# Which queue loads the second sequence's first keys and queries, and which one issues the last store

## The chip, the cores and the metric

The kernel runs on one core of one Trainium2 chip. A core has five engines with an instruction queue each: PE (TensorE: matrix products, into PSUM), DVE (VectorE), ACT (ScalarE), POOL (GpSimd) and SP (SyncE, which here only issues DMAs). DMAs are issued from SP and from POOL; a DMA issued from POOL can round fp32 to bf16 on its way, one from SP copies bytes as they are. The metric is the device time of one execution in microseconds, the median of several runs.

## The reference

Attention that looks at the best six key chunks of each query, followed by a two-layer network with a squared ReLU. Shapes: 4 sequences, 8 heads, 768 positions, 64 wide; network 512 to 2048 to 512.

```python
def _attn_ref(q, k, v):
    k_chunks = k.reshape(B, H, nc, chunk, D)              # nc = 24 chunks of 32 keys
    k_min, k_max = np.min(k_chunks, axis=3), np.max(k_chunks, axis=3)
    ub = np.sum(np.maximum(q[..., None, :] * k_min[:, :, None],
                           q[..., None, :] * k_max[:, :, None]), axis=-1)
    ub = np.where(causal, ub, -1e9)
    top_chunks = np.argsort(ub, axis=-1)[..., -6:]
    scores = scale * np.matmul(q, k.transpose(0, 1, 3, 2))
    ...
    scores = np.where(chosen & causal_mask, scores, -1e9)
    attn = softmax(scores)
    return np.matmul(attn, v)

def _moe_ref(x, w_in, w_out):
    h = np.maximum(x @ w_in, 0.0)
    return h * h @ w_out
```

`_attn_ref` and `_moe_ref` are cut here to what matters.

## The kernel before

**How the work is cut.** Each sequence is cut into blocks of 128 positions. The first block of every sequence has at most four chunks of keys in sight, so that it needs no selection; `first_transposes` and `first_attention` do it for all eight heads of a sequence at once. These four first blocks, one of each sequence, then go through the network together: `up(f, 0, 256, f)` for sequences 0 and 1, `up(f, 256, 512, f)` for 2 and 3, each for the first four column groups of w_in, then the rest. The other five blocks go by pairs of heads (16 pairs, `stage_a` for transposes, bounds and the choice of chunks, `stage_b` for scores and values, and other forms for the last sequence), and each sequence's five blocks then go through the network (`ffn`).

**What sets the order.** `Plan` takes every piece of work as an operation with a due date, the engines that could do it with an assumed cost each (`plan.op({"ACT": 0.48}, due, ...)`), what it needs, and the buffers it uses. `Plan.order` runs through time in a small model of the engines and of the transfers: among the operations that could start first it takes the one with the earliest due date, notes engine and start, and in the end writes all of them out in order of start. So the assumed costs and the times at which engines are first free (`free`) decide which engine does what and in which order; on the chip each engine then works its own list off in that order, and waits where an input is late. Where the model expects PE to wait in the opening, it writes filler products on the tile `warm`. Due dates come from formulas and from a list `moves` of shifts, each for a range of operations by number, that stands in `P`.

**The loads.** `P["sp"]` names the loads issued from SP, `'K0 Q0 K1 Q1'`: first blocks of keys and queries of sequences 0 and 1. `load_by_sp` (L496) loads them in fp32 into the tile `raw` (L500) and rounds them with a copy by DVE or ACT (L503, shown by the profile at the helper's L370). All other loads are issued from POOL by `load`, which rounds on the way: `load_first` (L461) for first blocks, `load_pair` (L553, shown at L555) for one head's other blocks, `load_w_in` (L560) for weights. Their list is `P["loads"]`: capital letters are first blocks (K2: keys of sequence 2), `k0` is a pair's keys, two loads, `i0` a quarter of w_in. `P["order"]` permutes the single loads of this list; the order issued is Q3, K2, V1, K3, V0, Q2, i0, V2, V3, then single loads of pairs. POOL issues a load only if the load eight before it has landed.

**Before the first load.** POOL makes `ident` (the identity for transposes) and `ahead` (a causal mask) and may set columns of ones in `vn` (`ones`, L520). `made["rows", 0]` (ACT, L432) writes rows that index the key chunks; `made["rows", 1]` to `[..., 7]` are copies of these by whichever engine is free (`kq_rows`, L429: POOL at L437, DVE and ACT by the helper `copy`, L368 and L370). With `after=1` in `P`, the first load is made to need the first of these copies:

```python
    if P["after"]:
        plan.loads[0].needs.append(made["rows", P["after"]])
```

**The stores.** `down` (L1189) makes one block's output `py`, copies it to `ob` (L368 or L370), and stores it (L1213) from SP, or from POOL for sequences 1 and 2. The last block is cut into columns 0 to 384 and 384 to 512, so that the last store is short.

Of the kernel before, what the change touches and what calls it, by code (L numbers as in the profile page):

```python
# [13 lines left out]
ACT = mybir.ActivationFunctionType  # L14
# [67 lines left out]
class Plan:  # L82
# [12 lines left out]
    NEVER = 1e9  # L95

# [22 lines left out]
    def order(self):  # L119
        free = {e: 0.7 for e in ("PE", "ACT", "DVE", "POOL", "SP")}  # L120
# [10 lines left out]
        landed, done, loads = [], [], 0  # L131
        rows = 128
        dma = Transfers()
        while ready:
# [34 lines left out]
            if engine == "PE":  # L169
# [9 lines left out]
                rows = op.rows  # L179
            op.engine, op.start, op.end = engine, st, st + cost  # L180
# [37 lines left out]
def kernel(  # L218
# [32 lines left out]
             -1393.33, -782.42, -326.54], sp='K0 Q0 K1 Q1', rows=[-2963.23,  # L251
             -1559.78, 780.78, -565.55, 1811.92, 457.36, -1818.66, -283.78],
             after=1, up_due=-65.96, up_rate=8.56, half=4, due=[-23.17,
# [3 lines left out]
             sel=2, loads='Q3 K3 V0 V1 Q2 K2 i0 V2 k0 V3 q0 i1 k1 v2 q1 i2 '  # L257
             'v0 i3 k2 q2 o1 o0 v1 o2 k3 o3 v3 q3')
    P.update(moves=[(702, 770, 14.04), (644, 759, -9.08), (940, 964, 20.66), (410,
# [1053 lines left out]
```

## Time and profile before

| what | us |
|---|---|
| median of 3 runs | 261.64 (261.3 to 263.74) |
| the profiled execution | 262.89 |
| its span, first to last instruction | 261.2 |
| SP's loads of queries and keys into raw, issue to landing, median | 4.0 and 4.4 |
| POOL's loads of w_in in the first 25 us, issue to landing, median | 7.7 |
| POOL's loads of v in the first 25 us, issue to landing, median | 6.7 |

The profile is that of one execution. A busy PE isn't PE at its peak, since products are pipelined and their ends modelled. Times in the order of time count from the span's start. A line such as L370 is that of the helper that records the instruction, so groups are told apart by their tiles: `q<-raw` is the rounding of SP's queries, `q<-in_q_dram` a load of a first block from POOL, `qn<-in_q_dram` one of a pair. DMA instructions show the time in which they are issued, not that of the transfer. PEclk 1.00 is the full clock.

### The profile page before, as it was taken

The page shows a single profiled execution, that of the slowest core. Times are in us where ns is not written, and L with a number is a line of the kernel's source. Part 1 is how long each engine was busy: PE and PEld are TensorE (multiplying, and loading weights), DVE is VectorE, ACT ScalarE, POOL GpSimd, SP SyncE. Part 2 cuts the span into 40 slices and gives each one's busy share as a digit, 9 for nine tenths or more (in the row PEclk, how much of TensorE's full clock was granted, in tenths as well). Part 3 has the DMA queues.
Part 4 walks back from the last instruction along what each step waited for, and adds up shares of the span by engine and source line. Part 5 has one row for each costly group of instructions (what it writes and reads, how often), then busy time and mean ns, then how long its engine had stood idle before and what let it go on. Part 6 is the DMA issues. An engine that isn't in the chain of part 4 may idle for free.

```text
span 261.2 us, 6709 instructions
## 1 busy us (share of the span) xinstructions
PE 249.4 (95%) x2471; PEld 160.3 (61%) x2471; DVE 191.0 (73%) x692; ACT 188.6 (72%) x379; POOL 115.2 (44%) x194
## 2 busy tenths in 40 slices
PE   6878899999999999999999999999999999999995
PEld 2547456666688666565678655656766554865443
DVE  6548999899999999998799972568979840555000
ACT  8545799685899999999988766776985821677112
POOL 7969988779758578832332031150003401000000
PEclk9599999999999999999999999999999999999999
DMA  8999999999999999991451753964797025200122
GB/s 157 138 159 148 168 181 169 183 139 183 170 211 137 145 109 173 152 166 23 77 163 28 162 74 94 207 116 103 175 184 118 17 72 136 82 0 4 40 80 80
DMA packets 117281, 32.16 MB, mean 123 GB/s; under 512 B 99840, under 2 KB 114944, under 8 KB 117248
## 3 DMA queue, kind: packets, MB, share of 16 engines
q0 software_dynamic: 75888, 15.73, 73.4%
q1 hardware_dynamic: 41360, 16.00, 31.4%
q8 instruction: 19, 0.31, 0.5%
q14 instruction: 14, 0.11, 0.2%
HBM read 32.77 MB, written 6.55 MB: 151 GB/s over the span
## 4 chain that ended last, share of the span: by engine, by line
PE 70%; DVE 11%; ACT 9%; DMA 4%; POOL 3%; issue 2%; ACTq 0%; POOLq 0%
PE py L1199 28%; PE ph L1168 25%; PE ps L1008 7%; PE av L1020 4%; ACT e L1032 4%; DMA v<-in_v_dram 4%; ACT kqc L368 4%; PE ps L1065 2%; DVE kqc L370 2%; PE av L1098 2%; DVE h L1186 2%; DVE kr L845 1%; DVE m L816 1%; DVE ht L1177 1%; POOL k L462 1%
## 5 line engine op out<-in xcount | busy, mean ns | idle before, releaser
L1168 PE MATMUL ph<-xT,w_in_sb 128*128 128x256 bf16 (+2 forms) x592 | 95.7, 304 | 1.7 <-DVE ht L1177 0.7
L1199 PE MATMUL py<-w_out_sb,h 128*128 128x512 bf16 (+2 forms) x400 | 91.6, 370 | 0.0
L1168 PEld LDWEIGHTS <-w_in_sb 128*128 128x128 bf16 x592 | 55.3, 97 | 25.9 <-issue 2.5
L1032 ACT ACTIVATE e<-ps 128x512 bf16<-128x512 f32 x120 | 64.9, 608 | 7.9 <-PE ps L1008 5.0
L1175 ACT ACTIVATE ht<-ph 128x384 bf16<-128x384 f32 (+2 forms) x120 | 53.3, 451 | 18.7 <-PE ph L1168 14.0
L1199 PEld LDWEIGHTS <-h 128*128 128x128 bf16 x400 | 36.2, 97 | 33.6
L1186 DVE TENSOR_TENSOR h<-ht 128x256 bf16<-128x256 bf16 (+2 forms) x148 | 47.6, 332 | 10.6 <-ACT ht L1175 8.2
L988 POOL TENSOR_SCALAR_AFFINE_SELECT e<-e 128x128 bf16<-128x128 bf16 (+1 forms) x66 | 24.4, 377 | 43.8 <-ACT e L1032 42.8
L1008 PE MATMUL ps<-kqc 88*128 88x128 bf16 (+1 forms) x240 | 39.4, 272 | 0.7 <-ACT e L1032 0.6
L368 ACT COPY ob<-py 128x512 f32<-128x512 f32 (+2 forms) x24 | 13.8, 575 | 29.2 <-PE py L1199 29.2
L1008 PEld LDWEIGHTS <-kqc 88*128 88x128 bf16 x240 | 19.8, 97 | 11.3 <-issue 1.1
L1020 PEld LDWEIGHTS <-e 128*128 128x128 bf16 x480 | 21.6, 97 | 4.5 <-POOL e L988 0.5
L1103 ACT ACTIVATE e<-ps 128x512 bf16<-128x512 f32 x40 | 21.5, 605 | 1.9 <-PE ps L1065 1.8
L1177 DVE TENSOR_SCALAR ht<-ph 128x256 bf16<-128x256 f32 (+2 forms) x28 | 13.7, 492 | 11.7 <-PE ph L1168 11.5
L1020 PE MATMUL av<-vn,e 128*128 128x65 bf16 x360 | 21.7, 193 | 0.0
L1213 POOL DMA_DIRECT2D out_dram<-ob x10 | 5.5, 553 | 33.8 <-ACT ob L368 33.8
L1112 DVE TENSOR_TENSOR e<-e,mask 128x512 bf16<-128x512 bf16 x40 | 17.4, 457 | 3.2 <-ACT e L1103 2.2
L716 DVE TENSOR_TENSOR x<-av,rc 128x320 bf16<-128x320 f32 (+1 forms) x40 | 18.6, 472 | 0.5
L988 POOL TENSOR_SCALAR_AFFINE_SELECT mask<-mask 128x256 bf16<-128x256 bf16 x20 | 9.2, 496 | 20.9 <-DVE x L716 12.5
L845 DVE TENSOR_REDUCE kr<-kT 128x24 bf16<-128x768 bf16 x16 | 14.8, 953 | 0.9 <-PE kT L373 0.8
L368 ACT COPY kqc<-sT 24x384 bf16<-24x384 bf16 (+1 forms) x27 | 11.7, 434 | 4.3 <-PE sT L373 2.6
L714 DVE RECIPROCAL rc<-av 128x5 f32<-128x5 f32 (+1 forms) x40 | 7.3, 187 | 9.4 <-PE av L1020 5.3
(115 smaller groups left out, 323.9 us busy)
## 6 DMA issues: line engine op xcount, KB each, us to landing
mask<-seen SPq DMA_DIRECT2D x16, 336.0 KB, 7.8
out_dram<-ob SPq DMA_DIRECT2D x13, 256.0 KB, 2.6
out_dram<-ob POOLq DMA_DIRECT2D x10, 256.0 KB, 2.9
w_in_sb<-in_moe_w_in_dram POOLq DMA_DIRECT2D x4, 512.0 KB, 7.6
w_out_sb<-in_moe_w_out_dram POOLq DMA_DIRECT2D x4, 512.0 KB, 9.0
vn<-in_v_dram POOLq DMA_DIRECT2D x15, 128.0 KB, 5.8
nt<-in_q_dram POOLq DMA_DIRECT2D x10, 128.0 KB, 6.1
nt<-in_k_dram POOLq DMA_DIRECT2D x10, 128.0 KB, 5.8
```

The lines of the kernel that those rows point to most:

```text
L368: nc.scalar.copy(dst, src)
L716: return plan.op({"DVE": 0.06 + 0.00108 * D * n}, due, lambda _: nc.vector.tensor_mul(x(), av[:, :, 0:D], rc[:, 0:n].unsqueeze(2).to_broad ...
L845: nc.vector.tensor_reduce(kr[:, mm].rearrange("d (t c) -> d t c", c=128 // CH) if b >= BY_DMA else kr[:, mm], part(kT).rearrange("d t (c j ...
L988: nc.gpsimd.affine_select(out=e, in_=e, compare_op=ALU.is_ge, fill=0.0, base=0, channel_multiplier=-1, pattern=[[0, n], [1, 128]])
L1008: nc.tensor.matmul(ps[:, 128 * c:128 * (c + nt)], lhsT=kqs(slice(0, KC), s, hh)[:, 128 * j:128 * (j + 1)], rhs=qss(slice(0, KC), s, hh)[:, ...
L1020: nc.tensor.matmul(av[:, t - 1], lhsT=e[:, 128 * c:128 * (c + 1)], rhs=value_tile(b, h, j), start=(i == 0 and c == 0), stop=(i == len(BANK ...
L1032: nc.scalar.activation(e.tile, ps.tile, ACT.Exp, scale=scale), [sc], [ps, e])
L1103: done = plan.op({"ACT": 0.48}, due + 0.5, lambda _: nc.scalar.activation(e.tile, ps.tile, ACT.Exp, scale=scale), [sc], [ps, e])
L1168: nc.tensor.matmul(ph.tile, lhsT=w_in_sb[:, ki, 128 * f:128 * (f + 1)], rhs=xT[:, c0 // 128:c1 // 128, ki], start=(ki == 0), stop=(ki == N ...
L1175: nc.scalar.activation(ht.tile, ph.tile, ACT.Relu)
L1186: {"DVE": 0.067 + w / 1920}, at[0] + P["h2"], lambda _: nc.vector.tensor_mul(h2[f][:, c0:c1], ht.tile, ht.tile), [op], [ht, h2[f]])))
L1199: nc.tensor.matmul(py.tile, lhsT=h2[f][:, 128 * t:128 * (t + 1)], rhs=w_out_sb[:, f, c0:c1], start=(f == 0), stop=(f == NFI - 1))
```

## The change

Keys and queries of sequence 1's first block (`K1`, `Q1`) go from SP's list to the head of POOL's, which rounds them on the way; their two copies on DVE or ACT go. `after=0`: the first load no longer needs a copy of the index rows. The last store is issued from ACT, the engine that can make the copy before it. The planner's assumptions are others: engines are first free at 0.8 to 2.0 us and not all at 0.7, the first two loads cost 0.34 and 0.18 us more, `ident`, `ahead` and `ubmask` have other costs, `wait` is 0.00419 and not 0.00328. `moves` and `order` are other lists, so the order of work is another on all engines, in the whole run. The order of loads becomes K1, Q1, Q3, V0, V1, K3, Q2, i0, K2, V3, one load of k0, V2, then single loads of pairs.

```diff
+    SLOW = (0.34, 0.18)
...
-        free = {e: 0.7 for e in ("PE", "ACT", "DVE", "POOL", "SP")}
+        free = {"PE": 0.9, "ACT": 2.0, "DVE": 0.9, "POOL": 1.0, "SP": 0.8}
...
+            if op.load and loads < len(self.SLOW):
+                cost += self.SLOW[loads]
...
-             -1393.33, -782.42, -326.54], sp='K0 Q0 K1 Q1', rows=[-2963.23,
+             -1393.33, -782.42, -326.54], sp='K0 Q0', rows=[-2963.23,
...
-             after=1, up_due=-65.96, up_rate=8.56, half=4, due=[-23.17,
+             after=0, up_due=-65.96, up_rate=8.56, half=4, due=[-23.17,
...
-             sel=2, loads='Q3 K3 V0 V1 Q2 K2 i0 V2 k0 V3 q0 i1 k1 v2 q1 i2 '
+             sel=2, loads='K1 Q1 Q3 K3 V0 V1 Q2 K2 i0 V2 k0 V3 q0 i1 k1 v2 q1 i2 '
...
-    P.update(moves=[(702, 770, 14.04), (644, 759, -9.08), (940, 964, 20.66), (410,
+    P.update(moves=[(698, 766, 15.28), (638, 753, -8.79), (938, 962, 18.75), (677,
...
-             order=[0, 5, 3, 1, 2, 4, 6, 7, 10, 9, 19, 12, 11, 8, 13, 14, 15, 16,
+             order=[0, 1, 2, 4, 5, 3, 6, 8, 7, 12, 11, 9, 21, 14, 13,
...
-             wait=0.00328)
+             wait=0.00419)
...
-    made["ident"] = plan.op({"POOL": 0.75}, -997, lambda _: make_identity(nc, ident))
-    made["ahead"] = plan.op({"POOL": 0.55}, -994, make_ahead)
+    made["ident"] = plan.op({"POOL": 0.60}, -997, lambda _: make_identity(nc, ident))
+    made["ahead"] = plan.op({"POOL": 0.45}, -994, make_ahead)
...
-    made["ubmask"] = plan.op({"DVE": 0.8}, -997, make_ubmask)
+    made["ubmask"] = plan.op({"DVE": 1.27}, -997, make_ubmask)
...
-            plan.op({"POOL": 0.80} if by_pool else {"SP": 0.35}, at[0] + 1, lambda e: (
-                nc.gpsimd if e == "POOL" else nc.sync).dma_start(
+            by = {"POOL": 0.80} if by_pool else {"ACT": 0.10} if c0 else {"SP": 0.35}
+            plan.op(by, at[0] + 1, lambda e: {
+                "POOL": nc.gpsimd, "ACT": nc.scalar, "SP": nc.sync}[e].dma_start(
                     out[rows[t]:rows[t] + 128, c0:c1], ob.tile), [op], [ob],
                 packets=2 * w, turns=not by_pool, free=by_pool)
```

Between `moves=` and `order=` both lists run on for dozens of lines of shifts.

More of the change, by code (lines that the diff above doesn't have):

```diff
@@ L256 @@
              'q3 v2 v3 k3', shift={}, p0=-2735.84, wait=0.01, xt=(1, 2, 3),
-             sel=2, loads='Q3 K3 V0 V1 Q2 K2 i0 V2 k0 V3 q0 i1 k1 v2 q1 i2 '
+             sel=2, loads='K1 Q1 Q3 K3 V0 V1 Q2 K2 i0 V2 k0 V3 q0 i1 k1 v2 q1 i2 '
              'v0 i3 k2 q2 o1 o0 v1 o2 k3 o3 v3 q3')
-    P.update(moves=[(702, 770, 14.04), (644, 759, -9.08), (940, 964, 20.66), (410,
[69 rows of a table removed]
-             order=[0, 5, 3, 1, 2, 4, 6, 7, 10, 9, 19, 12, 11, 8, 13, 14, 15, 16,
[4 rows of a table removed]
-             wait=0.00328)
+    P.update(moves=[(698, 766, 15.28), (638, 753, -8.79), (938, 962, 18.75), (677,
[110 rows of a table added]
+             463, -2.42)], order=[0, 1, 2, 4, 5, 3, 6, 8, 7, 12, 11, 9, 21, 14, 13,
[5 rows of a table added]
+             wait=0.00419)
     nc.scalar.preload_act_table_set("natural_log_exp_and_others")
```

188 rows, old and new, of tables (order, sel) are left out of this document.

## The prediction

> **What bounds the kernel now.** I read the page first, then busy time by stage, PE's waits, and the order of time of the opening.
>
> ```profile
> PE 249.4 (95%) x2471; PEld 160.3 (61%) x2471; DVE 191.0 (73%) x692; ACT 188.6 (72%) x379; POOL 115.2 (44%) x194
> PE 70%; DVE 11%; ACT 9%; DMA 4%; POOL 3%; issue 2%; ACTq 0%; POOLq 0%
> ```
>
> The first line is busy time, the second the chain that ended last. PE is busy for 249.4 of 261.2 us and carries 70% of the chain. A part of the change that doesn't give PE its work earlier, or shorten what stands behind PE's last matmul, gives nothing. Where PE has room is seen by stage; the first number of a row after the comma is PE's busy time, then PEld, DVE, ACT, POOL; the granted clock, the DMA share and GB/s end it.
>
> ```profile
> 0.00:3.80 3.80, 2.67 (x7) 1.02 (x8) 2.47 (x19) 2.95 (x4) 2.26 (x11) 1.00 0.49 111
> 3.80:7.20 3.40, 1.60 (x12) 0.56 (x10) 2.56 (x6) 3.26 (x5) 3.34 (x6) 1.00 1.50 208
> 7.20:10.60 3.40, 2.90 (x30) 1.85 (x31) 1.56 (x4) 1.68 (x4) 3.40 (x5) 0.54 2.09 133
> 10.60:14.00 3.40, 3.40 (x36) 2.55 (x36) 2.41 (x9) 1.07 (x2) 3.40 (x5) 0.50 1.68 145
> 14.00:17.40 3.40, 2.74 (x34) 1.71 (x32) 1.62 (x5) 2.17 (x4) 2.53 (x3) 0.96 1.74 161
> 17.40:20.80 3.40, 1.91 (x22) 1.60 (x23) 0.83 (x4) 0.77 (x2) 1.38 (x2) 1.00 2.09 153
> 20.80:24.20 3.40, 3.05 (x47) 2.65 (x46) 3.12 (x12) 2.37 (x5) 3.40 (x5) 1.00 1.64 177
> 24.20:130.00 105.80, 103.10 (x1106) 67.82 (x1105) 100.06 (x357) 93.23 (x183) 75.47 (x120) 1.00 1.70 149
> 130.00:258.00 128.00, 127.98 (x1191) 80.53 (x1188) 76.38 (x282) 80.83 (x173) 20.03 (x43) 1.00 0.44 97
> 258.00:261.20 3.20, 0.06 (x2) 0.00 (x0) 0.00 (x0) 0.27 (x1) 0.00 (x0) 0.82 0.24 82
> ```
>
> Up to 24.2 us PE is idle for 24.2 - 18.27 = 5.9 us, and for 6.8 us it runs at half clock. From 24.2 to 130 it is idle for 105.80 - 103.10 = 2.70 us, with VectorE at 100.06 beside it. From 130 to 258 nothing is left, and the last 3.2 us are the last store. So there is an opening, a middle with 2.7 us to give, and a tail.
>
> ```profile
> PE T L373 <- DVE q L370: 2.0, 2, 1.2
> PE sT L373 <- DVE selb L875: 0.8, 1, 0.8
> ```
>
> Two of PE's waits (us in total, times, longest): the largest of the opening is for VectorE's rounding of queries that SP loaded, the other is the largest of the middle. The opening in order of time (start, length, what, and in brackets the idle time before) shows two more waits of PE, for Pool's loads:
>
> ```profile
> 2.91 0.90 SPq L500 DMA_DIRECT2D raw<-in_k_dram  x1
> 1.59 0.29 POOL L413 TENSOR_SCALAR_AFFINE_SELECT ahead<-ahead 128x128 bf16<-128x128 bf16 x1
> 1.83 0.45 POOL L523 MEMSET vn<- 128x40 bf16 x2
> 3.07 0.82 POOL L437 TENSOR_SCALAR_AFFINE_SELECT kqc<-kqc 24x768 bf16<-24x768 bf16 x1 [0.79 <-ACT kqc L432]
> 4.02 1.20 POOL L462 DMA_DIRECT2D q<-in_q_dram  x1
> 5.21 1.04 POOL L462 DMA_DIRECT2D k<-in_k_dram  x1
> 6.25 0.88 POOL L462 DMA_DIRECT2D v<-in_v_dram  x1
> 9.71 0.80 POOL L562 DMA_DIRECT2D w_in_sb<-in_moe_w_in_dram  x1
> 6.56 0.82 DVE L370 CAST q<-raw 128x512 bf16<-128x512 f32 x1 [0.78 <-DMA raw<-in_q_dram]
> 7.72 0.53 DVE L370 CAST k<-raw 128x512 bf16<-128x512 f32 x1 [0.34 <-DMA raw<-in_k_dram]
> 8.85 0.61 PE L685 MATMUL ps<-t,t 64*128 64x128 bf16 x8
> 16.17 0.83 PE L641 MATMUL ph<-warm 128*128 128x256 bf16 x6
> 17.49 1.05 PE L1168 MATMUL ph<-xT,w_in_sb 128*128 128x256 bf16 x8 [0.49 <-DMA w_in_sb<-in_moe_w_in_dram]
> 19.94 0.40 PE L692 MATMUL av<-v,e 128*128 128x65 bf16 x8 [1.41 <-DMA v<-in_v_dram]
> ```
>
> Pool waits 0.79 us for ScalarE's first index rows, copies a set of them (0.82 us), and only then issues loads, one behind the other, from 4.02 us. The first weights are its seventh load; PE takes them at 17.49 us, with 0.83 us of filler on warm and 0.49 us of idleness before.
>
> **The change part by part.**
>
> Pool's first load, not held back: Pool ends ahead at 1.59 + 0.29 = 1.88 us, so the first load can start at 1.9 us, 2.1 us earlier. The index rows and the memsets that it did before (0.82 and 0.45) go to ScalarE or VectorE, or between the loads, where each delays every later load by its length.
>
> Two loads moved from SP to Pool: SP issues two of its four, Pool two more, ahead of all others. The first two loads cost 1.20 and 1.04 us whichever they are, later ones 0.88. The weights are then the eighth: 1.9 + 1.20 + 1.04 + 5 x 0.88 = 8.5 us instead of 9.71: 1.2 us earlier, or 0.4 if the copy of rows (0.82) stands between. Behind this the transfers must keep up:
>
> ```profile
> q1 hardware_dynamic: 1738, 0.44, 132.9%
> q0 software_dynamic: 2373, 0.30, 234.9%
> raw<-in_q_dram SPq DMA_DIRECT2D x2, 256.0 KB, 4.0
> q<-in_q_dram POOLq DMA_DIRECT2D x2, 128.0 KB, 4.3
> k<-in_k_dram POOLq DMA_DIRECT2D x2, 128.0 KB, 4.5
> ```
>
> The first two rows are packets in 4 to 6 us (SP's queue alone) and in 9 to 11 us (Pool's alone): 869 a microsecond against 1187. Two tensors of some 1024 packets take 2.36 us there and 1.73 here: 0.6 us less. The lead that weights and later loads get lies between 0.6 (transfers) and 1.2 us (issues); I take 0.9, their middle, as the two limits alternate.
>
> The Trainium skill speaks against this part: its page "DMA: Bandwidth & Descriptors", section "Issuing engine by pattern", gives simple loads to Sync as the generally faster issuer, and its section "Issuing engines are not separate DMA queues" says that another issuer saves only issue time, because all run on the same 16 engines. By that rule the sum would lose the 0.6 and, where Pool's issues aren't what limits, the lead. The trace agrees in the time to landing (4.0 against 4.3 us) and not in packets per microsecond, where SP's hold 253 bytes each (0.44 MB by 1738) and Pool's 126.
>
> VectorE's two casts go, 0.82 + 0.53 = 1.35 us. The second sequence's queries are ready at 7.38 and its keys at 8.25 us now; by Pool they are issued at 1.9 and 3.1 us and land, at 4.3 to 4.5 us each, at about 6.3 and 7.5 us. That moves the second sequence's transposes, and the scores of 8.85 us that stand behind them in PE's order, up by some 0.8 us. It is worth nothing by itself: the cover is the wait for weights at 17.49, over 8 us later. If that cover were gone it would be worth the 0.8.
>
> The new order of loads is read from the two lists; these rows price what it moves:
>
> ```profile
> 15.84 0.40 PE L685 MATMUL ps<-t,t 64*128 64x128 bf16 x8
> 8.96 0.42 DVE L370 COPY t<-T 128x512 bf16<-128x512 bf16 x1 [0.71 <-PE T L373]
> 16.27 1.09 ACT L701 ACTIVATE e<-ps 128x512 bf16<-128x512 f32 x2 [1.15 <-PE ps L685]
> 21.05 0.53 PE L692 MATMUL av<-v,e 128*128 128x65 bf16 x8
> 22.48 0.44 PE L373 MATMUL qT<-ident,qn 128*128 128x128 bf16 x5
> ```
>
> In the new order the third sequence's keys go from second place to behind the first weights, and its values behind those and a load of the pairs. Keys need more steps than values before an output: transposes, copy, scores, exponentials, some 2.35 us by 0.44, 0.42, 0.40 and 1.09 us. At the place where values land now (PE's wait ends at 19.94), less 0.9, they land at 19.0 and reach their values product at about 21.4, against 21.05 for the last of these products now (an estimate from these rows). So the second half of the first up-projection gains nothing, while the pairs, which keep their distance from the start of the stream, gain the 0.9; with them starts the first chain of bounds and selection, which ends in PE's 0.8 us wait for selb.
>
> Opening: -0.9, from -1.2 to +0.5 where the keys come late.
>
> The middle: due dates and costs of the planner are replaced, so the order of work on all engines changes, which no row shows. Below lies at most the 2.70 us of idleness; above, an order that fits badly can lose as much. Of the rows, the 0.8 us wait for selb is nearest to this change, since its chain starts with the loads: I take half of it, -0.4.
>
> The last store on ScalarE:
>
> ```profile
> 258.14 0.27 ACT L368 COPY ob<-py 128x128 f32<-128x128 f32 x1 [0.41 <-PE py L1199]
> 258.43 0.33 SPq L1213 DMA_DIRECT2D out_dram<-ob  x1
> ```
>
> ScalarE's copy ends at 258.41, SP issues at 258.43. Nothing else is queued on SP or ScalarE then, so a hand-over of 0.02 to 0.1 us is all that can go; a first issue on a queue not used before may cost up to what SP's dearest issue above exceeds this one (0.90 - 0.33 = 0.6). I take -0.1, nearest to the hand-over.
>
> Sum: -0.9 - 0.4 - 0.1 = -1.4 us. The profiled execution took 262.89 us (span 261.2 and 1.7 around it), the median of the runs is 261.64; 261.5 on the former's scale is 260.2 on the median's.
>
> **The rivals.** A: as summed, 260.2 us, from 259.0 to 261.3.
>
> B: the middle closes. The lead of 0.9 and VectorE's spared casts let the new order hide nearly all waits between 24.2 and 130: 2.3 of the 2.70 us go. For it: these waits are few and short (the largest 0.8). Against it: VectorE is busy 95% of that stretch (100.06 of 105.80), so it leaves little room to reorder. 261.64 - 0.9 - 2.3 - 0.1 = 258.3 us.
>
> C: the loads were hidden anyway. What is read from memory is the same, and what ends the opening is the last first block and the pairs, not the first weights. For it: the DMA share is 1.50 or more in each slice from 3.8 us on, and PE's longest wait of the opening is 1.41 us, for v behind those weights. Then only the store's 0.1 is left: 261.5 us. The Trainium skill's section on issuing engines ("DMA: Bandwidth & Descriptors") leads here too.
>
> D: slower, by the clock. The slice with 1.60 of 3.40 us busy was followed by two slices at 0.54 and 0.50; the one with 1.91 (17.4 to 20.8) was not. If the earlier weights let both pieces of 1.05 us run before 18.7 us and the late keys leave PE nothing until about 21, a slice falls under some 1.6, and the next 6.8 us run at half clock. PE has about 6.4 us of work there (3.05 of 3.40, then 103.10 of 105.80), so half of it, 3.2 us, is lost and nothing behind gives it back. 261.64 - 0.5 + 3.2 = 264.3 us. Against it: filler on warm is planned into such gaps (0.83 us at 16.17). The Trainium skill ("TensorE: Matmul & The Clock Gate", Part 1) has free-running windows of 3.4 us after which an idle one halves the clock; the two slow slices, 6.8 us, agree with windows of that length.
>
> **How the numbers follow.** About 1% (2.6 us) is what a measurement of this kernel can tell from no change: faster is under 259.0, slower over 264.3. Chances: A 0.40, B 0.25, C 0.18, D 0.17. Faster: 0.23 of B and 0.10 of A's lower end, 0.33. Slower: D with the upper half of what a badly fitting middle adds, 0.15. The rest, 0.52, is within. The range of 8 in 10 reaches from B with the rest of the middle (258.3 - 0.5 = 257.8) to D (264.4). A's own range is 259.0 to 261.3.
>
> **What would show it.** Right: Pool's first load at about 1.9 us, w_in at about 8.5, PE's first product with it by 16.6; casts of raw twice and not four times; PE's idle time up to 24.2 us under 5.2; the pairs' first transposes near 21.6 instead of 22.5 us. Wrong: w_in landing where it does now (C); a granted clock near 0.5 behind 17 us (D); PE idle between 24.2 and 130 us at more than 3.5 us, which would put the loss in the new order.

## The result and the profile after

| what | before | after |
|---|---|---|
| median, same chip, 14 runs each | 263.11 us (261.3 to 267.43) | 261.13 us (260.38 to 261.89) |
| ratio | 1 | 0.9937, 95% interval 0.9914 to 0.996 |
| the profiled execution | 262.89 us | 261.43 us |
| its span | 261.2 us | 259.7 us |

The changed kernel is faster by 0.63%: less than the 1% that the prediction took for a visible change, but the interval excludes 1. The ratio leaves out the run at 267.43 us, which was in a slower state of the chip, and it is not the quotient of the two medians, which is 0.9925. Against 261.64 us, the median that the prediction started from, 0.9937 is 260.0 us; the forecast was 260.2, a ratio of 0.9945.

The first lines of the page after, busy time and the chain that ended last:

```profile
PE 245.5 (95%) x2444; PEld 158.2 (61%) x2468; DVE 193.0 (74%) x705; ACT 188.7 (73%) x375; POOL 114.4 (44%) x185
PE 57%; DMA 18%; POOL 9%; DVE 8%; ACT 5%; issue 2%; POOLq 0%; ACTq 0%; DVEq 0%
```

PE is still what carries the run, at 95%. (The chain now names transfers where before it went on along PE. PE shows 2444 products, though 2468 weights were loaded: some records of products are missing from this trace. Its busy time is therefore not compared to the last us, and I go by the times at which the same step starts.)

The windows of the opening, with the same columns as before (PE, PEld, DVE, ACT, POOL, granted clock, DMA share, GB/s):

```profile
3.80:7.20 3.40, 1.98 (x20) 1.01 (x18) 1.52 (x7) 3.30 (x5) 3.40 (x5) 1.00 1.90 139
7.20:10.60 3.40, 2.67 (x42) 1.88 (x42) 2.20 (x7) 2.31 (x5) 3.40 (x5) 1.00 2.22 142
10.60:14.00 3.40, 2.38 (x34) 1.67 (x35) 2.55 (x9) 1.37 (x4) 3.40 (x5) 1.00 1.28 149
14.00:17.40 3.40, 2.54 (x24) 1.86 (x23) 0.54 (x3) 1.25 (x3) 2.42 (x4) 1.00 2.25 163
```

Between 7.2 and 14 us the granted clock is 1.00, where it was 0.54 and 0.50. The prediction had not forecast that; whether it is part of the gain is asked below. The order of time, with Pool's loads first, then PE's steps that answer to the rows shown of before:

```profile
1.59 0.29 POOL L458 TENSOR_SCALAR_AFFINE_SELECT ahead<-ahead 128x128 bf16<-128x128 bf16 x1
1.90 1.05 POOL L507 DMA_DIRECT2D k<-in_k_dram  x1
2.95 1.89 POOL L507 DMA_DIRECT2D q<-in_q_dram  x2
4.82 1.77 POOL L507 DMA_DIRECT2D v<-in_v_dram  x2
6.55 0.91 POOL L507 DMA_DIRECT2D k<-in_k_dram  x1
7.42 0.92 POOL L507 DMA_DIRECT2D q<-in_q_dram  x1
8.29 0.80 POOL L607 DMA_DIRECT2D w_in_sb<-in_moe_w_in_dram  x1
15.94 1.05 PE L1213 MATMUL ph<-xT,w_in_sb 128*128 128x256 bf16 x8 [0.86 <-DMA w_in_sb<-in_moe_w_in_dram]
16.82 0.39 PE L418 MATMUL T<-ident,k 128*128 128x128 bf16 x4
19.75 0.41 PE L737 MATMUL av<-v,e 128*128 128x65 bf16 x8 [0.99 <-DVE x L761]
20.74 0.44 PE L418 MATMUL qT<-ident,qn 128*128 128x128 bf16 x5 [0.36 <-DMA qn<-in_q_dram]
```

The first load starts at 1.90 us, right behind ahead, and the weights are issued at 8.29 instead of 9.71. Everything that hangs on the stream of loads is earlier by nearly the same: PE's first product with the weights at 15.94 instead of 17.49 (1.55 us) and the pairs' first transposes at 20.74 instead of 22.48 (1.74 us). The end of the run, in order of time:

```profile
256.50 0.27 ACT L413 COPY ob<-py 128x128 f32<-128x128 f32 x1 [0.41 <-PE py L1244]
256.80 0.38 ACTq L1259 DMA_DIRECT2D out_dram<-ob  x1
```

The last copy starts at 256.50 instead of 258.14, 1.64 us earlier. So the lead that the opening has at 16 to 21 us (1.55 to 1.74) is the lead at the end: what lies between adds nothing that these two traces show. (Other traces below show that a lead can get lost on the way.)

### The profile page after: what moved, and what is told of

It reads as the page before. It is cut to its first block, busy times and chain, and to the rows that moved or that the text cites. A ratio compares the mean times of both kernels' runs of the same rounds, so it can differ in the third digit from the quotient of the medians.

```text
span 259.7 us, 6670 instructions
## 1 busy us (share of the span) xinstructions
PE 245.5 (95%) x2444; PEld 158.2 (61%) x2468; DVE 193.0 (74%) x705; ACT 188.7 (73%) x375; POOL 114.4 (44%) x185
## 3 DMA queue, kind: packets, MB, share of 16 engines
HBM read 32.77 MB, written 6.55 MB: 151 GB/s over the span
## 4 chain that ended last, share of the span: by engine, by line
PE 57%; DMA 18%; POOL 9%; DVE 8%; ACT 5%; issue 2%; POOLq 0%; ACTq 0%; DVEq 0%
PE py L1244 23%; PE ph L1213 22%; DMA qt<-nt 5%; DMA nt<-in_q_dram 5%; DMA w_out_sb<-in_moe_w_out_dram 5%; PE ps L1053 4%; DMA w_in_sb<-in_moe_w_in_dram 3%; PE av L1065 2%; DVE kr L890 2%; ACT e L1077 2%; PE ps L1110 2%; PE av L1143 2%; ACT kqc L413 2%; DVE h L1231 2%; POOL vn L593 1%
## 5 line engine op out<-in xcount | busy, mean ns | idle before, releaser
L1244 PE MATMUL py<-w_out_sb,h 128*128 128x512 bf16 (+2 forms) x376 | 88.3, 370 | 1.2
L1220 ACT ACTIVATE ht<-ph 128x256 bf16<-128x256 f32 (+2 forms) x117 | 52.1, 452 | 19.8 <-PE ph L1213 15.3
L1231 DVE TENSOR_TENSOR h<-ht 128x256 bf16<-128x256 bf16 (+2 forms) x148 | 46.8, 329 | 12.8 <-ACT ht L1220 10.2
L1053 PE MATMUL ps<-kqc 88*128 88x128 bf16 (+1 forms) x240 | 38.7, 272 | 0.1
L1033 POOL TENSOR_SCALAR_AFFINE_SELECT e<-e 128x128 bf16<-128x128 bf16 (+1 forms) x58 | 23.2, 414 | 33.7 <-ACT e L1077 29.8
L413 ACT COPY ob<-py 128x512 f32<-128x512 f32 (+2 forms) x21 | 11.9, 569 | 28.2 <-PE py L1244 28.2
L1065 PEld LDWEIGHTS <-e 128*128 128x128 bf16 x480 | 21.4, 97 | 5.4 <-POOL e L1033 1.8
L1222 DVE TENSOR_SCALAR ht<-ph 128x256 bf16<-128x256 f32 (+2 forms) x31 | 15.0, 484 | 11.0 <-PE ph L1213 10.6
L1033 POOL TENSOR_SCALAR_AFFINE_SELECT mask<-mask 128x256 bf16<-128x256 bf16 x20 | 9.8, 523 | 29.8 <-DMA mask<-seen 18.0
L1259 POOL DMA_DIRECT2D out_dram<-ob x10 | 5.6, 556 | 35.8 <-ACT ob L413 33.0
L1030 DVE TENSOR_TENSOR e<-e,tri 128x128 bf16<-128x128 bf16 (+1 forms) x38 | 8.7, 236 | 10.3 <-ACT e L1077 9.8
```

Of the source, the lines that this page charges most:

```text
L413: nc.scalar.copy(dst, src)
L1033: nc.gpsimd.affine_select(out=e, in_=e, compare_op=ALU.is_ge, fill=0.0, base=0, channel_multiplier=-1, pattern=[[0, n], [1, 128]])
L1053: nc.tensor.matmul(ps[:, 128 * c:128 * (c + nt)], lhsT=kqs(slice(0, KC), s, hh)[:, 128 * j:128 * (j + 1)], rhs=qss(slice(0, KC), s, hh)[:, ...
L1065: nc.tensor.matmul(av[:, t - 1], lhsT=e[:, 128 * c:128 * (c + 1)], rhs=value_tile(b, h, j), start=(i == 0 and c == 0), stop=(i == len(BANK ...
L1220: nc.scalar.activation(ht.tile, ph.tile, ACT.Relu)
L1231: {"DVE": 0.067 + w / 1920}, at[0] + P["h2"], lambda _: nc.vector.tensor_mul(h2[f][:, c0:c1], ht.tile, ht.tile), [op], [ht, h2[f]])))
```

## The experiments

Three theories stood against each other: that the gain is **the loads' lead** (both load edits), that it is **the new order of work** on the engines, and that it is **PE's clock**, which no longer falls to half in the opening. All ratios are to the kernel before, run on the same chip beside the experiment; brackets are 95% intervals.

### The two load edits in the order of before

`b_early` takes away only what held Pool's first load back. Pool's copy of the index rows goes behind 14 loads:

```diff
-        for op in self.order():
+        ops = self.order()
+        held = [op for op in ops if op in self.copies and op.engine == "POOL"
+                and op.start < self.loads[0].start]
...
+        at = ops.index(self.loads[14])
+        ops[at:at] = held
```

> The kernel before with its own order on every engine; only Pool's copy of the index rows goes from ahead of its first load to ahead of its fifteenth, so that the loads start at about 2.0 to 2.4 us instead of 4.02. Theory 1 (the lead of Pool's stream of loads is what the change gains, and it reaches the end whole): the first weights reach PE at 15.5 to 16.5 us instead of 17.49, and the time falls by 0.9 to 1.5 us, ratio to before 0.994 to 0.997. Theory 2 (the new order of work on the engines is the gain; the loads were hidden anyway): ratio 0.999 to 1.001.

`b_pool` only moves K1 and Q1 from SP to the head of Pool's loads, which stay held back; the two copies of raw go:

```diff
+            if op is self.loads[0]:
+                self.ahead()
...
+    def second_by_pool():
+        for nm in "kq":
+            nc.gpsimd.dma_start(out=first_of(nm, 1), in_=SRC[nm][1, :, 0:128].rearrange(
+                "h p d -> p h d"))
```

> The kernel before with its own order; only the second sequence's first keys and queries are loaded by Pool, ahead of its other loads, and their two casts on VectorE go. Pool is still held back until 4.02 us. Theory 1: the weights are the ninth load and are issued some 1.8 us later, at about 11.5 us, and reach PE at 18.5 to 19.3; the time rises by 1.0 to 1.8 us, ratio 1.004 to 1.007. Theory 2: no change, 0.999 to 1.001, or less if the casts were in the way (0.997).

`b_both` has both edits, with the order of loads of before behind K1 and Q1, so that w_in is the ninth load.

> The kernel before with its own order, both edits to the loads together, neither the new order of work nor the store by ScalarE. Theory 1: nearly the whole gain of the change, the time falls by 1.0 to 1.6 us, ratio 0.994 to 0.996. Theory 2: ratio 0.999 to 1.001.

Measured: b_early 261.73 us, 0.9977 [0.9951, 1.0002]; b_pool 264.04, 1.0059 [1.0035, 1.0084]; b_both 261.74, 0.9985 [0.996, 1.0011]. None has the gain of the change, and b_pool is slower.

In b_early the order of time shows who pays for Pool's earlier start (VectorE's roundings of sequence 1, then PE):

```profile
2.08 1.05 POOL L469 DMA_DIRECT2D q<-in_q_dram  x1
7.74 0.78 POOL L569 DMA_DIRECT2D w_in_sb<-in_moe_w_in_dram  x1
6.41 0.72 DVE L377 CAST q<-raw 128x512 bf16<-128x512 f32 x1 [0.18 <-DMA raw<-in_q_dram]
9.08 0.57 DVE L377 CAST k<-raw 128x512 bf16<-128x512 f32 x1 [1.95 <-DMA raw<-in_k_dram]
9.71 0.61 PE L380 MATMUL T<-ident,k 128*128 128x128 bf16 x4 [2.12 <-DVE k L377]
18.11 1.04 PE L1176 MATMUL ph<-xT,w_in_sb 128*128 128x256 bf16 x8
```

The weights are issued 1.97 us earlier than before (7.74 against 9.71) and PE takes them 0.62 us later (18.11 against 17.49), without waiting for them: no idle time stands behind that row. It is late with the first blocks: VectorE can round SP's second tensor of keys only at 9.08, not 7.72. Pool's transfers now run beside SP's, and SP's loads of keys take 5.1 us from issue to landing (median of two) instead of 4.4; that the one causes the other is likely, not tested apart. The Trainium skill ("DMA: Bandwidth & Descriptors", section "Issuing engines are not separate DMA queues") has all issuers' transfers interleave on the same 16 engines; this 1.36 us agrees.

In b_pool the first load starts at 4.02 us, as before, and two loads stand ahead of the old stream: w_in is issued at 11.44 us. PE's row:

```profile
9.26 0.61 PE L375 MATMUL T<-ident,q 128*128 128x128 bf16 x4 [1.21 <-DMA q<-in_q_dram]
18.48 1.05 PE L1177 MATMUL ph<-xT,w_in_sb 128*128 128x256 bf16 x8
```

Moving the loads without starting earlier puts 1.73 us (11.44 - 9.71) into the stream and makes sequence 1 late as well (its transposes at 9.26 instead of 7.44).

In b_both sequence 1 is no longer late, but w_in is issued at 9.47, where it was before:

```profile
17.55 1.05 PE L1185 MATMUL ph<-xT,w_in_sb 128*128 128x256 bf16 x8 [1.15 <-DMA w_in_sb<-in_moe_w_in_dram]
```

PE takes the weights at 17.55 against 17.49, now with 1.15 us of idleness ahead of it: two more loads ahead of w_in used up the earlier start. My expectation missed this; it had taken the early start as a lead for every load.

The opening is not the whole account of these runs. In b_pool PE starts the pairs' first transposes at 22.56 us and in b_both at 21.47, against 22.48 before; yet b_pool's span is 1.6 us longer than that of before, and b_both's 1.01 us of lead don't reach its end. Later in both traces PE waits 1.0 us for VectorE's product of exponentials and mask, which it doesn't in the traces of before and of b_early (b_both's row of PE's waits; it is at 172.55 us):

```profile
PE av L1115 <- DVE e L1129: 1.0, 1, 1.0
```

So in the order of before a lead can be lost again behind the opening. Why VectorE is late there stays open, and each trace is one execution: b_both's took 263.49 us, 1.75 more than its median.

### The two load edits undone in the changed kernel

`a_held` brings a copy of the index rows, made by VectorE in the changed kernel, back to Pool ahead of its first load. `a_sp` gives K1 and Q1 back to SP and rounds them by VectorE just before their transposes. `a_held_sp` does both, so that only the new order of work and loads (and the store) is left of the change.

```diff
-        for op in self.order():
+        ops = self.order()
+        one = min((op for op in self.copies if op.engine == "DVE"), key=lambda op: op.start)
...
+        one.engine = "POOL"
+        at = ops.index(self.loads[0])
+        ops[at:at] = [self.rows0, one]
```

```diff
-        load((nm, b, "first"), lambda _: nc.gpsimd.dma_start(
-            out=first_of(nm, b),
+        by_sp = b == 1 and nm in "kq"
+        load((nm, b, "first"), lambda _: (nc.sync if by_sp else nc.gpsimd).dma_start(
+            out=raws[nm].tile[:, b] if by_sp else first_of(nm, b),
...
+            if b == 1:
+                nc.vector.tensor_copy(first_of(nm, b), raws[nm].tile[:, b])
```

The first diff is a_held, the second a_sp.

> The changed kernel with its new order on every engine, but Pool held back again: before its first load it waits for ScalarE's first index rows and copies a set of them, which VectorE no longer does. Theory 1: all loads come 2.0 us later, the weights reach PE at about 17.9 us, the time rises by 1.5 to 2.0 us, ratio to before 0.999 to 1.002. Theory 2: it keeps the gain, 0.993 to 0.995.

> The changed kernel with its new order, but the second sequence's first keys and queries loaded by SP in fp32 and rounded by VectorE right before their transposes. Pool's other loads are issued some 2.0 us earlier, and SP's four loads take 0.6 us more of transfers. Theory 1 by issues: weights at PE up to 1 us earlier, ratio 0.990 to 0.993. Theory 1 by transfers (the stream is limited by the transfers, Pool's issues aren't the limit): 0.0 to 0.6 us slower than the changed kernel, ratio 0.994 to 0.996. Theory 2: the casts cost VectorE 1.35 us early, 0.994.

> The changed kernel with both edits to the loads undone: the new order of work and of loads, and the store by ScalarE, alone. Theory 1: no gain is left, ratio 0.998 to 1.002. Theory 2: the gain stays, 0.993 to 0.995.

Measured: a_held 264.56 us, 1.0087 [1.0055, 1.0119]; a_sp 263.74, 1.0064 [1.0041, 1.0086]; a_held_sp 262.4, 1.0006 [0.9982, 1.003].

The new order of work alone is worth nothing that can be measured. a_held is a miss: it is slower than before, where I had expected no more than the gain to go. Pool's load and PE's first product with it:

```profile
10.11 0.82 POOL L614 DMA_DIRECT2D w_in_sb<-in_moe_w_in_dram  x1
19.66 1.91 PE L1222 MATMUL ph<-xT,w_in_sb 128*128 128x256 bf16 x8
```

w_in is issued only 0.40 us later than before (10.11 against 9.71), but PE comes to it 2.17 us later and without waiting for it. It had waited 1.16 us for queries at 15.62, and its granted clock was 0.62, 0.50 and 0.50 in the three windows from 10.6 to 20.8 us.

And a_sp, where I expected most of the gain to stay, is slower than before, though its weights are the earliest of all. The order of time of Pool's load, VectorE's rounding and PE:

```profile
6.55 0.79 POOL L608 DMA_DIRECT2D w_in_sb<-in_moe_w_in_dram  x1
9.82 0.43 DVE L707 CAST q<-raw 128x512 bf16<-128x512 f32 x1 [1.35 <-DMA raw<-in_q_dram]
10.31 0.61 PE L418 MATMUL T<-ident,q 128*128 128x128 bf16 x4 [1.38 <-DVE q L707]
17.76 1.04 PE L1216 MATMUL ph<-xT,w_in_sb 128*128 128x256 bf16 x8
```

w_in is issued at 6.55 us, 1.74 us before the changed kernel's, but PE comes to it at 17.76, 1.82 us later. It waited 1.38 us for sequence 1's queries, which SP loads beside Pool's stream. Once the weights come early, sequence 1's keys and queries are the limit. It is the same reading as b_early's. It explains that the gain is gone, not that a_sp is slower than before: its pairs' first transposes start at 22.01, still 0.47 us ahead of before, and the traced execution, 262.78 us, is the fastest of its six.

### The last store

`a_store_sp` is the changed kernel with that store issued by SP again (one word in L1259).

> The changed kernel with the last store issued by SP again, at the same place. All theories: within 0.15 us of the changed kernel, ratio to before 0.993 to 0.9945. From the end of the last copy to the end of the span it is 2.76 us before and 2.92 us in the changed kernel; if the store by ScalarE costs, this run shows 2.8 or less, if it is chance 2.9 or any.

Measured: 261.29 us, 0.9959 [0.9935, 0.9984]; the changed kernel's 0.9937 lies in that interval. From the end of the last copy to the end of the span it was 261.2 - 258.41 = 2.79 us before, with SP, and 259.7 - 256.77 = 2.93 after, with ScalarE. In a_store_sp it is 260.0 - 257.11 = 2.89, so by the expectation the difference is chance. Over all traces SP's tails are 2.75 to 2.92 us and ScalarE's 2.85 to 2.97. The store by ScalarE gains nothing that these runs show.

### Pool's first load earlier still

`a_load_first` puts the first load ahead of ident and ahead in Pool's order.

```diff
-        for op in self.order():
+        ops = self.order()
+        for op in self.loads[0:1]:
+            ops.remove(op)
+            ops.insert(ops.index(self.ident), op)
```

> The changed kernel with Pool's first load moved ahead of the identity and the mask that Pool makes: it starts at about 0.9 us instead of 1.90, the others follow 0.2 to 0.5 us earlier, since those two then stand behind it. Theory 1: 0.2 to 0.5 us faster than the changed kernel, ratio 0.992 to 0.993. Rival: the identity comes 1 us later, ScalarE's index rows and casts with it, and the first sequence's scores; hidden behind the weights it changes nothing, 0.9937; not hidden, up to 1 us slower, 0.9975.

Measured: 262.03 us, 1.0009 [0.9983, 1.0035]: a miss, and the change's gain is gone. Pool's and ScalarE's rows, then PE's:

```profile
1.34 1.02 POOL L511 DMA_DIRECT2D k<-in_k_dram  x1 [0.82 <-POOLq L1349]
3.50 1.81 POOL L511 DMA_DIRECT2D q<-in_q_dram  x2
2.98 0.84 ACT L481 ACTIVATE kqc<-ident 24x768 bf16<-24x768 bf16 x1 [0.88 <-POOL ident masks.py:199]
5.43 0.62 ACT L417 CAST q<-raw 128x512 bf16<-128x512 f32 x1
6.11 0.40 PE L422 MATMUL T<-ident,q 128*128 128x128 bf16 x4 [0.92 <-ACT q L417]
```

One load gains 0.56 us; the second starts at 3.50 instead of 2.95, because ident and ahead now stand between. ScalarE waits 0.88 us for ident, rounds sequence 0's queries at 5.43 instead of 4.55, and PE's first transposes start at 6.11 instead of 5.22. PE takes the weights at 16.48 instead of 15.94. So a place ahead of ident doesn't pay. These rows don't show the whole of it, though: the traced execution is the fastest of the twelve (260.59 us), with a span of 258.9 us against 259.7 of the changed kernel's.

### PE's clock, and the place of the weights

Four kernels ran together on one chip. `b_warm` is the kernel before with twelve filler products on warm ahead of each of the first sequences' transposes; `a_cold` is the changed kernel without its filler before 10 us; `a_k2_front` puts the third sequence's keys back ahead of the weights; `a_again` is the changed kernel.

```diff
+        turns = sorted(self.turns, key=lambda op: op.start)
+        turns[0].fill = turns[2].fill = 3
```

```diff
-            if op.fill:
+            if op.fill and op.start > 10:
```

```diff
+        ops.remove(self.loads[8])
+        ops.insert(ops.index(self.loads[3]), self.loads[8])
```

These are b_warm, a_cold and a_k2_front, in this order.

> The kernel before with more filler products on the tile warm ahead of PE's first transposes of sequence 0 and of sequence 1, and nothing else; loads and order as before. Theory 'PE's clock is a share of the gain': the granted clock no longer falls to half between 7.2 and 14 us; the weights still land near 17.4 us and PE's first product with them stays there, and what is gained is only that the first sequences' scores are through earlier. Ratio to the kernel before 0.997 to 0.999. Were the clock the whole of the gain: 0.994 to 0.996. Theory 'all of the gain is the weights' lead': 0.999 to 1.001.

> The changed kernel without its planned filler products before 10 us; loads and order as in the changed kernel. Theory 'PE's clock is a share of the gain': the granted clock falls to about half in two slices between 7 and 17 us, PE's first product with the weights starts 0.5 to 2 us later than 15.94, and the ratio to the kernel before is 0.996 to 1.000. Theory 'all of the gain is the weights' lead': the weights still land near 15.9 and the ratio stays at 0.993 to 0.996.

> The changed kernel with the third sequence's first keys issued as the fourth load again, ahead of the weights, which become the ninth load; the order of work on the other engines as in the changed kernel. Theory 'the weights' lead is the gain': w_in is issued some 0.87 us later, PE's first product with it starts at 16.6 to 17.0 instead of 15.94, and 0.3 to 0.9 us of the gain go: ratio 0.996 to 0.9985. Theory 'the place of the keys of sequence 2 doesn't matter, the loads' start at 1.9 us is the gain': 0.9935 to 0.996. If the keys' late place costs something, as the prediction had it: 0.990 to 0.993.

> The changed kernel as it is, on the same chip as the other three. Every theory: 0.9915 to 0.996, weights taken by PE at 15.9 to 16.2 us, granted clock at 1.0 throughout.

Measured: b_warm 263.13 us, 1.0015 [0.9993, 1.0036]; a_cold 261.62, 0.9967 [0.9942, 0.9992]; a_k2_front 261.76, 0.9983 [0.9958, 1.0007]; a_again 261.94, 0.996 [0.9935, 0.9986].

In b_warm the windows between 7.2 and 14 us are at full clock, as they are after the change:

```profile
7.20:10.60 3.40, 2.87 (x44) 2.20 (x44) 1.36 (x5) 2.26 (x5) 3.40 (x5) 1.00 2.18 139
10.60:14.00 3.40, 2.47 (x34) 1.43 (x33) 3.22 (x11) 1.79 (x4) 3.40 (x5) 1.00 1.61 136
```

And 11 of its 12 runs had a mean clock of 0.998 or more, against 5 of 35 runs of the kernel before beside it. The time isn't better. (The fillers have a price of their own: PE's first transposes start at 6.12 instead of 5.50. By 8.90, at the scores, that is made up: 8.85 before.) The traced execution is the twelfth: its clock falls in the next two windows, and PE takes the weights only at 18.07:

```profile
14.00:17.40 3.40, 2.33 (x25) 1.56 (x26) 0.85 (x2) 0.58 (x2) 2.42 (x3) 0.83 1.78 174
17.40:20.80 3.40, 3.40 (x29) 2.65 (x27) 1.05 (x5) 1.57 (x5) 2.32 (x3) 0.67 2.13 148
```

So b_warm shows no gain from the full clock in the order of before. PE still waits for the weights there (0.49 us in the trace of before), so that being there earlier is of no use.

For the changed kernel a_cold doesn't exclude the clock. Its clock falls to 0.86 and 0.64 in the windows from 10.6 to 17.4, and PE takes the weights at 16.78, 0.84 us later than in the changed kernel's trace and without the wait of 0.86 us. By its expectation that, with a ratio of 0.9967, is what the theory of a share foretold; but the span is 259.6 us, as short as the changed kernel's, and the ratio can't be told from a_again's. The single runs say more. This is their mean time by the mean granted clock of the run (the rows are from different chips):

| kernel | runs at 0.998 or more | runs below |
|---|---|---|
| before, beside these four | 5: 262.59 us | 29: 262.60 (a thirtieth took 265.13) |
| before, beside b_early | 5: 261.93 | 24: 262.48 |
| b_warm | 11: 263.06 | 1: 263.50 |
| changed, first measurement | 11: 261.07 | 3: 261.43 |
| a_again | 5: 261.29 | 7: 262.39 |
| a_store_sp | 6: 261.24 | 4: 261.55 |
| a_cold | 3: 261.30 | 9: 262.01 |
| a_k2_front | 7: 261.48 | 5: 262.69 |
| a_held_sp | 3: 261.16 | 9: 262.66 |
| a_held and a_sp | none | 13: from 262.78 to 266.1 |

In the new order the runs that keep the clock take 261.1 to 261.5 us, even with both load edits undone, the others 0.3 to 1.5 us more, and a_held and a_sp never keep it. (a_load_first doesn't fit: 262.26 in 4 runs and 262.43 in 8.) How often PE keeps its clock may so be a part of what the load edits gain there. That is not shown: a late load can make PE wait and lower the clock as well, and no run here separates the two.

Behind the weights a lower clock costs time in one trace. a_again is the same program as the changed kernel, but in its profiled run the weights landed late:

```profile
16.70 1.56 PE L1213 MATMUL ph<-xT,w_in_sb 128*128 128x256 bf16 x8 [1.94 <-DMA w_in_sb<-in_moe_w_in_dram]
18.48 1.91 PE L1213 MATMUL ph<-xT,w_in_sb 128*128 128x256 bf16 x8
22.51 0.44 PE L418 MATMUL qT<-ident,qn 128*128 128x128 bf16 x5
```

```profile
14.00:17.40 3.40, 1.46 (x12) 1.00 (x11) 0.00 (x0) 0.17 (x1) 1.66 (x3) 0.95 2.29 158
17.40:20.80 3.40, 3.40 (x28) 2.32 (x26) 1.21 (x4) 1.52 (x4) 3.21 (x5) 0.55 1.77 126
```

The first of these fences is the order of time, the second the windows. w_in was issued at 8.29 in both runs; PE waited 1.94 us for it instead of 0.86, was busy for 1.46 us of that window, and the next window was granted at 0.55. A lateness of 0.76 us (16.70 against 15.94) became 1.77 us at the pairs' first transposes (22.51 against 20.74), and the span was 261.3 instead of 259.7. Of the lead over before nothing is left in that run: 22.51 against 22.48 at the pairs. My expectation, 15.9 to 16.2 us and full clock throughout, missed it. It is the rival D of the prediction, in one window and not two. The Trainium skill ("TensorE: Matmul & The Clock Gate", Part 1) has free-running windows of 3.4 us and a clock that is either full or half. The two rows agree: 0.05 and 0.45 below the full 1.00 add up to the 0.50 that one window at half clock takes away.

a_k2_front does what its edit says: w_in is issued at 9.13, and PE takes it at 17.07 after a wait of 1.18 us. Its interval overlaps a_again's almost wholly, and by the medians (0.18 us apart) it is the faster of the two, by the ratios the slower. The pairs' loads keep their place in it, and PE's first transposes of pairs start at 21.32. What the place of the weights alone is worth stays open.

### Read together

The ratios, by order of work and by the two load edits (the changed kernel stands at the lower right, with its repetition):

| order of work | held, K1 and Q1 by SP | early, by SP | held, by Pool | early, by Pool |
|---|---|---|---|---|
| before | 1 | 0.9977 | 1.0059 | 0.9985 |
| new | 1.0006 | 1.0064 | 1.0087 | 0.9937, 0.996 |

In the new order each load edit alone makes the kernel slower, and both together make it faster: their effects don't add. With the early start alone, SP's loads of sequence 1 run beside Pool's stream and land later; with the move alone, the stream is longer. The traces show both delays, but not that they make up the whole of the times. Shown is that the changed order needs both edits. That both need the new order is likely, not shown: b_both's interval, 0.996 to 1.0011, overlaps a_again's. The gain itself was largest in the first measurement: a_again and a_store_sp, the same kernel but for the last store, came out at 0.996 later.

## Why the prediction held, point by point

**Pool's first load at 1.9 us, the copy of rows off Pool.** Right: 1.90. **The weights' issue at 8.5.** Nearly: 8.29, since the two dearer loads cost 1.05 and about 1.0 us (1.89 for two, 0.88 of it for the third load), not 1.20 and 1.04.

**The lead of 0.9 us.** The mechanism was right and the term too small. Taken was the middle between 0.6 (transfers) and 1.2 us (issues); the traces show 1.55 at the weights and 1.74 at the pairs. The issues gave 1.42 of it. That step drew the lead down towards a limit by transfers that did not show in this run; a_again's run, with the weights at 16.70 (0.79 us earlier than before), shows that the middle is not absurd either. The lead varies from run to run.

**K1 and Q1 by Pool "worth nothing by itself".** As an edit by itself it was worse than nothing, b_pool's 1.0059. And the cover named, the wait for the weights, is gone as soon as the weights come early: a_sp and b_early show PE late with sequence 1's blocks and not waiting for weights. The sentence "if that cover were gone it would be worth the 0.8" was the right one, and the price too low: in the new order and with the early start, K1 and Q1 by SP (a_sp) give 1.0064, by Pool 0.9937 and 0.996. The step compared with SP's loads as they run in before (ready at 7.38 and 8.25), not as they run beside an early stream, where the later of the two is rounded at 9.08 (b_early) and 9.82 (a_sp).

**The third sequence's keys behind the weights: nothing gained for the second half.** Wrong. Its transposes started at 16.82, not after 19.0, and its values product at 19.75, not 21.4; what PE waited for there was VectorE (0.99 us), not a load. The second half of the up-projection, the products that wait 0.34 us for ScalarE's copy of xT, came forward by 1.43 us, from 23.82 to 22.39 (the order of time of before, then of after):

```profile
23.82 0.38 PE L1168 MATMUL ph<-xT,w_in_sb 128*128 128x256 bf16 x2 [0.34 <-ACT xT L368]
```

```profile
22.39 0.82 PE L1213 MATMUL ph<-xT,w_in_sb 128*128 128x256 bf16 x6 [0.34 <-ACT xT L413]
```

The step's estimate had let the keys land at the place of the values of before; the load right behind w_in was there for PE 0.88 us after it (16.82 against 15.94).

**The middle, -0.4.** Not there. The wait for selb is still 0.9 us (0.8 before):

```profile
PE sT L418 <- DVE selb L920: 0.9, 1, 0.9
PE ph L1213 <- DMA w_in_sb<-in_moe_w_in_dram: 0.9, 1, 0.9
```

The lead at the end is the opening's, and a_held_sp, the new order without the load edits, is at 1.0006. **The last store, -0.1.** Not there either: 2.93 us of tail against 2.79.

The sum, -1.4, met the profiled execution's -1.46 because the lead was undersized by 0.65 to 0.84 us, and the two gains that did not come made 0.5 of it up. That the number fits so well is luck: errors of opposite sign cancelled. By the ratio the change is worth 1.65 us of 261.64.

Of the signs named, the loads' start, the two casts left, and PE's first product before 16.6 came true, and the pairs were earlier still (20.74, not 21.6). PE's idle time between 24.2 and 130 us is 105.80 - 102.59 = 3.21 us, under the 3.5 named. One sign failed: PE's idle time up to 24.2 us was to fall under 5.2 us and rose from 5.9 to 24.2 - 17.13 = 7.1. Up to then PE ran 186 products in 17.13 us instead of 178 in 18.27, at a mean clock of 1.00 instead of 0.86. The prediction worked with the half clock as given, and so did not see that PE would be done with the first sequences early and wait longer for the weights (0.86 us instead of 0.49).

**The rivals.** C, the loads hidden anyway, fell: the weights and the pairs are early, and the issue order is worth time. Giving Pool two more loads costs 0.6% by itself (b_pool) and pays together with the early start in the new order (a_sp against the changed kernel); by the traces of a_sp and b_early what pays is that SP's two loads no longer run beside a stream that starts earlier. The rule of the Trainium skill that led to C ("DMA: Bandwidth & Descriptors", section "Issuing engine by pattern": simple loads to Sync) agrees with b_pool and not with the whole change. B fell with the middle. D, the lower clock, was seen behind the weights in a_again's trace, in one window, and costs about 1 us by a_again's runs, not 3.2; 7 of a_again's 12 runs and 3 of the changed kernel's 14 had a mean clock below 0.998.

## What to carry to other kernels

Two loads on different queues that look independent can delay each other: price a moved load by when the others land beside it, and test two load edits together and apart, since in the new order each alone made the kernel slower and both together made it faster. "Worth nothing, it is covered" holds only for the limit that stands now; when the same change removes that limit, price the covered step as the next limit. A lowered clock cost little or nothing here where a wait for the weights stood behind it (before); where none was left (a_held) or where it fell behind the wait (a_again) it went with lost time. So look at what PE does in the windows after, before adding filler. And split the single runs by their clock before a median is put down to an edit.

## What the runs showed of the hardware

How long PE counts as busy in a window can't be read as a threshold of the clock. The same twenty products between 3.8 and 7.2 us stand with 1.98 us in the changed kernel's profile (above) and with 3.25 us in a_again's, both at full clock:

```profile
3.80:7.20 3.40, 3.25 (x20) 1.63 (x18) 1.48 (x7) 3.30 (x5) 3.40 (x5) 1.00 1.94 146
```

Even the first four transposes of queries stand with 0.40 us in the one and 0.61 in the other. And a window with 1.89 us (a_held, 7.2 to 10.6) was followed by one at 0.62, while before one with 1.91 was followed by 1.00. So the limit of 1.6 us that rival D rested on is not to be had from such rows; that a window with 1.46 us was followed by 0.55 is what was seen.

The same program issued w_in at 8.29 us in two runs, and PE got it at 15.94 in one and at 16.70 in the other: the spread of one transfer from run to run is nearly half of this change's gain.

SP's two loads of queries into raw took 5.1 us from issue to landing beside the early stream of a_sp, against 4.0 before, those of keys 4.9 against 4.4. DMA issues of a_sp, whose last column is the median from issue to landing:

```profile
raw<-in_q_dram SPq DMA_DIRECT2D x2, 256.0 KB, 5.1
raw<-in_k_dram SPq DMA_DIRECT2D x2, 256.0 KB, 4.9
```
